# Where the high and low parts of rotated queries and keys are formed in a fused attention and MoE kernel

## Chip, cores and metric

The kernel runs on one core of a Trainium2 chip. The metric is the device time of one execution in microseconds (us), as a median over runs. Engines are named as in the profile: PE (TensorE; PEld is its weight load), DVE (VectorE), ACT (ScalarE), POOL (GpSimd), SP (SyncE, here only a queue of DMA issues).

## What is computed

Three stages follow each other. Attention with rotary embedding over 4 batches, 8 heads, 576 positions and head size 64; then a two-matrix MoE layer; then a gated one (SiLU). All is float32.

```
q_rot, k_rot = (rotate(q), rotate(k))
scores = scale * np.matmul(q_rot, k_rot.transpose(0, 1, 3, 2))
...
return np.matmul(attn, v).astype(np.float32)
...
h = x @ w_in
g = s * (np.maximum(h, 0.0) ** 2) + b
x = g @ w_out
...
silu = g * (1.0 / (1.0 + np.exp(-g)))     # g = x @ w_gate
return (silu * val @ w_out).astype(np.float32)   # val = x @ w_val
```

## The kernel before

Every matmul that must keep float32 accuracy is made from a high part (the value rounded to fp32r) and a low part (value minus high part), and the products high x high, high x low and low x high are summed in PSUM. So each operand is split once: one operation rounds it, a second subtracts.

The 32 heads are worked in 16 pairs. For each pair `prep(p)` makes the operands and `pair(p)` computes. `prep` loads q and k of two heads side by side into a tile `x` (two buffers; 128 x 1152 float32) and rotates them with four GpSimd operations (L486, L488, L491, L494, tile `ry` for the products). Then, in G = 3 groups of 384 columns, TensorE transposes the rotated rows into a PSUM bank `pst` (L514, nine transposes a pair; pool `t` of three banks, which the transposes of the probabilities, `ps_t`, use too). After a transpose the queries lie on partitions 0 to 63 and the keys on 64 to 127; a scale per partition (`qs`) gives the queries their factor. For pairs 2 to 15 each group's bank is read twice: ACT writes the rounded high part into `qkhi` (L523), and DVE subtracts it from the scaled bank into `qklo` (L525), which frees the bank. `qkhi` and `qklo` have one buffer each. Ten DMAs of SP then spread the two tiles into the operands `a`, `t` and `kz` of that pair (L547; two buffers of each, by parity of the pair), and only when they have landed may the next pair's high part be written. Pairs 0 and 1 take another way (L533, L536), which stays as it is.

`pair(p)` has nine units. Each computes scores of 128 rows on TensorE (`ps_s`, L619), a maximum on DVE (L622), and the exponential on ACT (L626). Three units make a third: their probabilities are transposed (L680, L683, banks `ps_t`), split into `ph` on ACT (L688) and `pl` on DVE (L695), and multiplied with the values (L710, L712), which GpSimd split (L569, L571, tile `vh`, three buffers). ACT takes the sum out (L723), and SP stores it (L731).

A pair has 40 score matmuls, 45 transposes of probabilities, 36 products with the values and 9 transposes of q and k: 130 on TensorE. Weights of the first MoE stage are loaded during attention and decoded (ACT L304, DVE L307, L310, L315) and split (ACT L342, GpSimd or DVE L349): the first WA = 10 of them have slots beside attention and their low part is GpSimd's; WB = 22 further slots open when attention is over.

The order of work on each engine is written out by a planner when the program is built: operations carry a duration, a priority (a smaller number first) and tokens for buffers, and `Schedule.run` plays them forward in planned time. On the chip every engine then runs its list strictly in that order, and an instruction whose semaphores are not there yet holds all that is behind it. The planner also keeps DVE operations marked `port=True` (the weight decode among them) from running while GpSimd is planned to be busy, and the other way round.

Of the kernel before, what the change touches and what calls it, by code (L numbers as in the profile page):

```python
# [8 lines left out]
F32 = mybir.dt.float32  # L9
# [21 lines left out]
class Schedule:  # L31
# [17 lines left out]
    def op(self, eng, dur, fn, prio, deps=(), acq=(), rel=(), lag=0.0, port=False):  # L49
        o = Op()  # L50
        o.size, o.next = None, []
        o.eng, o.dur, o.lag, o.fn, o.prio, o.port = eng, dur, lag, fn, prio, port
        o.acq, o.rel, o.users, o.ready, o.done = acq, rel, [], 0.0, None
        for t in rel:
            t.left += 1
        o.need = 0
        for d in set(d for d in deps if d is not None):
            d.users.append(o)
            o.need += 1
        self.ops.append(o)  # L60
        return o
# [116 lines left out]
def tile_attention_moe_moe(  # L178
# [26 lines left out]
    NU = PC  # L205
    QA = PC // 2
    UBS = (512, 512, 512, 384, 384)
    WA = 10
    WB = 22
    NE = 7  # L210
    LATE, LAST = 1 << 20, 1 << 21
    WARM = 75
# [9 lines left out]
    sch = Schedule()  # L222
    op = sch.op
    sch.free.update({
        "raw": 3, "dec": 2, "wa": WA, "x": 2, "vr": 2, "ry": 1, "hi": 1, "vh": 3, "opb0": 1, "opb1": 1, "l": 2, "lb": 2, "cr": 1, "e": NE, "ph": 2, "pl": 2,
        "xr": 2, "rbx": 1, "s": 2, "t": 3, "v": 1, "xhb": 1, "gb": 2, "rb2": 3,
    })

# [19 lines left out]
    ld_p = att.enter_context(tc.tile_pool(name="ld", bufs=2))  # L248
    vr_p = att.enter_context(tc.tile_pool(name="vr", bufs=2))
    rp_p = att.enter_context(tc.tile_pool(name="rp", bufs=1))  # L250
    v_p = att.enter_context(tc.tile_pool(name="v", bufs=3))
    ph_p = att.enter_context(tc.tile_pool(name="ph", bufs=2))
    pl_p = att.enter_context(tc.tile_pool(name="pl", bufs=2))
# [170 lines left out]
    def prep(p):  # L424
# [34 lines left out]
        def taken(ps):  # L459
            return ps[:, 0:CG].rearrange("p (h s) -> p h s", h=2)  # L460

        for g in range(G):
            cs = slice(g * PC // G, (g + 1) * PC // G)
            eng = "dve" if p == 0 else "pool"
            e = nc.vector if eng == "dve" else nc.gpsimd
            tt = t_dve if eng == "dve" else t_pool
            wide = [128, PC // G, 2, D // 2]
            def views(a, cs=cs):
                return st["x"].rearrange("p c j (a d) -> p c j a d", a=2)[:, cs, :, a], st["ry"][:, cs, :, a]
            def r0(g=g, e=e, views=views, cs=cs, wide=wide):  # L470
                if g == 0:
                    st["ry"] = rp_p.tile([128, PC, 2, 2, D // 2], F32, tag="ry", name="ry")
                e.tensor_tensor(out=views(0)[1], in0=views(1)[0], in1=rt[:, cs, 2:3].to_broadcast(wide), op=ALU.mult)
            def r1(e=e, views=views, cs=cs, wide=wide):
                e.tensor_tensor(out=views(1)[1], in0=views(0)[0], in1=rt[:, cs, 1:2].to_broadcast(wide), op=ALU.mult)
            def r2(e=e, cs=cs):
                xv = st["x"].rearrange("p c j (a d) -> p c (j a) d", a=2)[:, cs]
                e.tensor_tensor(out=xv, in0=xv, in1=rt[:, cs, 0:1].to_broadcast([128, PC // G, 4, D // 2]), op=ALU.mult)
            def r3(e=e, cs=cs):
                xv = st["x"].rearrange("p c j d -> p c (j d)")[:, cs]  # L480
                e.tensor_tensor(out=xv, in0=xv, in1=st["ry"].rearrange("p c j a d -> p c (j a d)")[:, cs], op=ALU.add)
            o = st.get("rope")
            if o is None and p:
                def y0():
                    st["ry"] = rp_p.tile([128, PC, 2, 2, D // 2], F32, tag="ry", name="ry")
                    nc.gpsimd.tensor_tensor(out=views2(0)[1], in0=views2(1)[0], in1=rt[:, :, 2:3].to_broadcast(whole), op=ALU.mult)  # L486
                def y1():
                    nc.gpsimd.tensor_tensor(out=views2(1)[1], in0=views2(0)[0], in1=rt[:, :, 1:2].to_broadcast(whole), op=ALU.mult)  # L488
                def y2():
                    xv = st["x"].rearrange("p c j (a d) -> p c (j a) d", a=2)  # L490
                    nc.gpsimd.tensor_tensor(out=xv, in0=xv, in1=rt[:, :, 0:1].to_broadcast([128, PC, 4, D // 2]), op=ALU.mult)  # L491
                def y3():
                    xv = st["x"].rearrange("p c j d -> p (c j d)")
                    nc.gpsimd.tensor_tensor(out=xv, in0=xv, in1=st["ry"].rearrange("p c j a d -> p (c j a d)"), op=ALU.add)  # L494
                n2 = PC * D
                for y, fn in enumerate((y0, y1, y2, y3)):
                    o = op("pool", t_pool(n2 if y < 2 else 2 * n2), fn, pr, (o, *lds[0], *rt_op), (ry_tok,) if y == 0 else (), (ry_tok,) if y == 3 else ())
                st["rope"] = o
            elif not p:
              o = None  # L500
              for y, fn in enumerate((r0, r1, r2, r3)):
                deps = [o, *lds[g], rt_op[g]]
                if y == 0 and g > 0:
                    deps.append(st["first"])
                o = op(eng, tt(fd if y > 1 else fd // 2), fn, pr + g, deps, (ry_tok,) if y == 0 and g == 0 else (),
                       (ry_tok,) if y == 3 else (), port=eng == "dve")
                if y == 0 and g == 0:
                    st["first"] = o
            ps_tok = Token("t")
            def tr(g=g):  # L510
                st["ps", g] = ps = ps_t.tile([128, 512], F32, tag="t", name="pst")
                rv = st["x"].rearrange("p c j d -> p c (j d)")
                for c in range(PC // G):
                    nc.tensor.transpose(taken(ps)[:, :, c * 64:(c + 1) * 64], rv[:, g * (PC // G) + c], ident.rearrange("p (h r) -> p h r", h=2))  # L514
            acq = (ps_tok, hi_tok if p > 1 else tok) if g == 0 else (ps_tok,)
            prt = pr + 3 + g
            o = st["tr"] = op("pe", 0.33, tr, prt, (o, eye_op, st.get("tr"), *(zeros[z] if p < 2 else ())), acq, (x_tok,))
            if p > 1:
                def hi(g=g):
                    if g == 0:  # L520
                        st["hi"] = rp_p.tile([128, 2 * S], F32R, tag="hi", name="qkhi")
                        st["lo"] = rp_p.tile([128, 2 * S], F32R, tag="lo", name="qklo")
                    nc.scalar.activation(out=place(st["hi"], g), in_=taken(st["ps", g]), func=AF.Copy, scale=qs_t)  # L523
                def lo(g=g):
                    nc.vector.scalar_tensor_tensor(  # L525
                        out=place(st["lo"], g), in0=taken(st["ps", g]), scalar=qs_t, in1=place(st["hi"], g).bitcast(F32), op0=ALU.mult, op1=ALU.subtract
                    )
                o = st["hi0"] = op("act", t_act(CG, True, 1), hi, prt, (o, qs_op, st.get("hi0")))
                trs.append(op("dve", t_dve(CG, 2), lo, prt, (o,), (), (ps_tok,)))
            else:  # L530
                def act(dst, rows, g=g):
                    scale = D ** -0.5 if rows is up else 1.0
                    return lambda: nc.scalar.activation(out=place(dst, g), in_=taken(st["ps", g])[rows], func=AF.Copy, scale=scale)  # L533
                def sub(dst, src, rows, g=g):
                    scale = D ** -0.5 if rows is up else 1.0
                    return lambda: nc.vector.scalar_tensor_tensor(  # L536
                        out=place(dst, g), in0=taken(st["ps", g])[rows], scalar=scale, in1=place(src, g).bitcast(F32), op0=ALU.mult, op1=ALU.subtract
                    )
                o1 = op("act", t_act(CG), act(t[dn], dn), prt, (o,))
                o2 = op("act", t_act(CG), act(a[up], up), prt, (o,))  # L540
                ops += [o1, o2, op("dve", t_dve(CG), sub(a[dn], a[up], up), prt, (o2,), (), (ps_tok,))]
                ops.append(op("act", t_act(CG), act(kz[up], dn), prt, (o,), (), (ps_tok,)))
                ops.append(op("dve", t_dve(CG), sub(t[up], t[dn], dn), prt, (o1,), (), (ps_tok,)))
        if p > 1:
            def sp(o, i, first=False):
                return sch.dma(
                    256 * o.shape[1], lambda: nc.sync.dma_start(out=o.bitcast(F32), in_=i().bitcast(F32)), pr + 6, (*trs, *zeros[z]),  # L547
                    (tok,) if first else (), (hi_tok,), pace=1.3
                )
# [821 lines left out]
```

## Time and profile before

| | |
|---|---|
| median of 3 runs | 1133.07 us (1133.0 to 1134.01) |
| span of the profiled execution, first to last instruction | 1130.5 us |
| mean granted clock of TensorE over the span | 0.995 of full speed |
| scores of pair 0 start, of pair 15 end | about 14 us, about 303 us |

The profile shows one execution from its first to its last instruction. Of that execution only the span is known; the median of the runs is 2.6 us above it, the time around the instructions.

### The profile page before, as it was taken

The numbers are of one execution on the slowest core, as the hardware profiler recorded it, in microseconds if no ns is written. First come the engines' busy times: TensorE is split into PE (matmuls) and PEld (weight loads), VectorE is DVE, ScalarE is ACT, GpSimd is POOL, SyncE is SP. The second block draws the span as 40 slices with busy tenths as digits, with TensorE's granted clock in tenths as the row PEclk, the third lists the DMA queues.
The fourth block names the chain that finished last, engine by engine and source line by source line (L and its number), as shares of the span: only waits on it lengthen the run. The fifth ranks groups of instructions, "written<-read, shape, count | busy, mean of one in ns | idle before, by whom it ended". The sixth has DMA issues, their size and how long they took to land. (4 is left out here: it accounts for less than half of the span.)

```text
span 1130.5 us, 17993 instructions
## 1 busy us (share of the span) xinstructions
PE 1103.6 (98%) x6314; PEld 1006.8 (89%) x6314; DVE 801.2 (71%) x1391; ACT 591.0 (52%) x1199; POOL 193.0 (17%) x156
## 2 busy tenths in 40 slices
PE   8989989999999999999999999999999999999998
PEld 7889888989988788888899999999979999899986
DVE  5879788999979867868768764555565555655560
ACT  5979888889978845544554543322242222422230
POOL 6876775752210000000000000000000000000000
PEclk9899999999999999999999999999999999999999
DMA  5587978777375477576576766766646652666501
GB/s 117 128 208 175 240 184 213 175 184 185 89 235 185 128 227 235 177 238 225 198 241 212 254 224 207 245 204 204 210 160 220 196 195 97 196 229 197 181 10 46
DMA packets 185721, 211.16 MB, mean 187 GB/s; under 512 B 71824, under 2 KB 121120, under 8 KB 185632
## 3 DMA queue, kind: packets, MB, share of 16 engines
q1 hardware_dynamic: 183792, 209.23, 61.8%
q8 instruction: 50, 0.82, 0.3%
q10 hardware_dynamic: 1840, 0.79, 0.2%
q14 instruction: 39, 0.32, 0.1%
HBM read 142.07 MB, written 47.26 MB: 167 GB/s over the span
## 5 line engine op out<-in xcount | busy, mean ns | idle before, releaser
L1241 DVE TENSOR_TENSOR tmp<-hb,tmp 128x384 f32<-128x384 f32 x252 | 140.0, 557 | 113.3 <-PE hb L811 112.4
L811 PE MATMUL hb<-xh,w 128*128 128x384 f32 (+1 forms) x560 | 199.2, 356 | 1.0 <-DVE w L349 1.0
L809 PE MATMUL hb<-xh,w 128*128 128x384 f32 (+1 forms) x560 | 199.0, 355 | 0.3 <-DVE pl L695 0.3
L810 PE MATMUL hb<-xl,w 128*128 128x384 f32 (+1 forms) x560 | 198.8, 355 | 0.0
L809 PE MATMUL acc<-gh,w 128*128 128x512 f32 (+1 forms) x320 | 117.8, 368 | 0.0
L810 PE MATMUL acc<-gl,w 128*128 128x512 f32 (+1 forms) x320 | 117.6, 368 | 0.0
L811 PE MATMUL acc<-gh,w 128*128 128x512 f32 (+1 forms) x320 | 117.6, 367 | 0.0
L622 DVE TENSOR_REDUCE nm<-ps_s 128x1 f32<-128x576 f32 x144 | 108.0, 751 | 9.8 <-PE ps_s L619 8.6
L809 PEld LDWEIGHTS hb<-xh,w 128*128 128x128 f32 x560 | 105.1, 188 | 10.9 <-PE ps_t L683 0.5
L810 PEld LDWEIGHTS hb<-xl,w 128*128 128x128 f32 x560 | 105.1, 188 | 10.3
L811 PEld LDWEIGHTS hb<-xh,w 128*128 128x128 f32 x560 | 105.1, 188 | 9.8 <-DVE w L349 1.8
L626 ACT ACTIVATE e<-ps_s,nm 128x576 f32<-128x576 f32 x144 | 107.3, 746 | 8.4 <-DVE nm L622 7.8
L688 ACT ACTIVATE ph<-ps_t 128x512 fp32r<-128x512 f32 x192 | 106.2, 574 | 10.1 <-PE ps_t L680 7.8
L619 PE MATMUL ps_s<-t,a 128*128 128x288 f32 x320 | 101.2, 332 | 7.2 <-ACT e L626 7.0
L710 PE MATMUL ps_av<-ph,vh 128*128 128x384 f32 (+1 forms) x320 | 97.9, 327 | 0.7 <-ACT xr L723 0.6
L695 DVE TENSOR_TENSOR pl<-ps_t,ph 128x512 fp32r<-128x512 f32 x144 | 95.9, 683 | 2.5 <-ACT ph L688 1.4
L1256 ACT ACTIVATE tmp<-tmp 128x384 f32<-128x384 f32 x72 | 37.8, 525 | 111.1 <-DVE tmp L1241 108.9
L680 PE MATMUL ps_t<-ident,e 128*128 128x128 f32 x576 | 87.7, 279 | 5.6 <-DVE qklo L525 4.0
L619 PE MATMUL ps_s<-kz,a 128*128 128x288 f32 x320 | 90.8, 299 | 0.0
L810 PE MATMUL hb<-w 128*128 128x384 f32 x264 | 88.9, 337 | 0.0
L811 PE MATMUL hb<-w 128*128 128x384 f32 x264 | 88.8, 337 | 0.0
L809 PE MATMUL hb<-w 128*128 128x384 f32 x264 | 88.5, 335 | 0.0
(117 smaller groups left out, 2304.2 us busy)
## 6 DMA issues: line engine op xcount, KB each, us to landing
w<-wd SPq DMA_DIRECT2D x120, 512.0 KB, 4.3
wd<-w SPq DMA_DIRECT2D x48, 512.0 KB, 3.6
raw<-in_moe_w_out_dram SPq DMA_DIRECT2D x28, 512.0 KB, 4.1
x_d<-xr SPq DMA_DIRECT2D x64, 144.0 KB, 2.7
w<-wd SPq DMA_DIRECT2D x36, 256.0 KB, 3.6
raw<-in_moe_w_in_dram SPq DMA_DIRECT2D x16, 512.0 KB, 4.4
raw<-in_moe_w_gate_dram SPq DMA_DIRECT2D x12, 512.0 KB, 5.5
raw<-in_moe_w_val_dram SPq DMA_DIRECT2D x12, 512.0 KB, 6.6
```

Source lines behind the costliest of these rows:

```text
L619: nc.tensor.matmul(ps[:, hf * 512:hf * 512 + HS], a[:, q0:q0 + 128], m[:, k0:k0 + HS], start=y == 0, stop=y == len(todo) - 1)
L622: nc.vector.tensor_reduce(out=st["nm"][:, u:u + 1], in_=st["s", u], axis=AX.XY, op=ALU.max, negate=True)
L626: nc.scalar.activation(out=st["e", u].rearrange("p (f n) -> p f n", f=2), in_=st["s", u], func=AF.Exp, bias=st["nm"][:, u:u + 1], accum_ou ...
L680: nc.tensor.transpose(ps[:, z * 128:z * 128 + 128], st["e", u][:, kc * 128:kc * 128 + 128], ident)
L688: nc.scalar.activation(out=st["ph", y][0:rows, 512 * i:512 * i + n], in_=st["pt", y, i][0:rows, 0:n], func=AF.Copy)
L695: nc.vector.tensor_tensor(out=dst, in0=st["pt", y, i][0:rows, 0:n], in1=st["ph", y][0:rows, c].bitcast(F32), op=ALU.subtract)
L710: nc.tensor.matmul(ps, vv, st["ph", y][:, c], start=kc == 0, stop=kc == 4)
L809: nc.tensor.matmul(o, lh, rh, start=first, stop=False)
L810: nc.tensor.matmul(o, lh, rl, start=False, stop=False)
L811: nc.tensor.matmul(o, ll, rh, start=False, stop=last)
L1241: nc.vector.tensor_tensor(out=st[dst, f], in0=ps[z], in1=st[a, f], op=ALU.add)
L1256: nc.scalar.activation(out=st[key, f], in_=st[key, f], func=AF.Silu)
```

## The change

For pairs 2 to 15 a transposed group leaves PSUM by one operation instead of two. It multiplies by `qs` and writes plain float32 back over the group's own columns of the tile `x`, which have just been transposed: on ACT for groups 0 and 2, on DVE for group 1. When the three groups are there, GpSimd makes the high part of all 1152 columns with one operation and the low part with another; the tile `x` is given back after the second, not after the transposes. `qkhi` and `qklo` get a pool of their own with two buffers each, and the token for a buffer is now taken by GpSimd's first operation, not by the first transpose. The scratch for DMA descriptors, which lies in SBUF, is set to 1 KB, and in the room so gained WA goes from 10 to 11 (WB, in the room that attention leaves, from 22 to 24).

```
-    WA = 10
-    WB = 22
+    WA = 11
+    WB = 24
...
-        "raw": 3, "dec": 2, "wa": WA, "x": 2, "vr": 2, "ry": 1, "hi": 1, ...
+        "raw": 3, "dec": 2, "wa": WA, "x": 2, "vr": 2, "ry": 1, "hi": 2, ...
...
+    hi_p = att.enter_context(tc.tile_pool(name="hi", bufs=2))
...
-            acq = (ps_tok, hi_tok if p > 1 else tok) if g == 0 else (ps_tok,)
+            acq = (ps_tok, tok) if g == 0 and p < 2 else (ps_tok,)
             prt = pr + 3 + g
-            o = st["tr"] = op("pe", 0.33, tr, prt, (...), acq, (x_tok,))
+            o = st["tr"] = op("pe", 0.33, tr, prt, (...), acq, (x_tok,) if p < 2 else ())
             if p > 1:
-                def hi(g=g):
-                    ...
-                    nc.scalar.activation(out=place(st["hi"], g), in_=taken(st["ps", g]), func=AF.Copy, scale=qs_t)
-                def lo(g=g):
-                    nc.vector.scalar_tensor_tensor(
-                        out=place(st["lo"], g), in0=taken(st["ps", g]), scalar=qs_t, in1=place(st["hi"], g).bitcast(F32), op0=ALU.mult, op1=ALU.subtract
-                    )
-                o = st["hi0"] = op("act", t_act(CG, True, 1), hi, prt, (o, qs_op, st.get("hi0")))
-                trs.append(op("dve", t_dve(CG, 2), lo, prt, (o,), (), (ps_tok,)))
+                def back(g=g):
+                    dst = st["x"].rearrange("p c j d -> p (c j d)")[:, g * CG:(g + 1) * CG]
+                    if g == 1:
+                        nc.vector.tensor_scalar(out=dst, in0=st["ps", g][:, 0:CG], scalar1=qs_t, scalar2=None, op0=ALU.mult)
+                    else:
+                        nc.scalar.activation(out=dst, in_=st["ps", g][:, 0:CG], func=AF.Copy, scale=qs_t)
+                dur = t_dve(CG, 1) if g == 1 else t_act(CG, True, 1)
+                trs.append(op("dve" if g == 1 else "act", dur, back, prt, (o, qs_op), (), (ps_tok,)))
...
         if p > 1:
+            def hi():
+                st["hi"] = hi_p.tile([128, 2 * S], F32R, tag="hi", name="qkhi")
+                st["lo"] = hi_p.tile([128, 2 * S], F32R, tag="lo", name="qklo")
+                nc.gpsimd.tensor_scalar(out=parts(st["hi"]), in0=val(), scalar1=1.0, scalar2=0.0, op0=ALU.mult, op1=ALU.add)
+            def lo():
+                nc.gpsimd.tensor_tensor(out=parts(st["lo"]), in0=val(), in1=parts(st["hi"]).bitcast(F32), op=ALU.subtract)
+            o = op("pool", t_pool1(2 * S), hi, pr + 5, trs, (hi_tok,))
+            trs = [op("pool", t_pool(2 * S), lo, pr + 5, (o,), (), (x_tok,))]
...
-    nc = _bacc.Bacc("TRN2", target_bir_lowering=False, num_devices=1)
+    nc = _bacc.Bacc("TRN2", target_bir_lowering=False, num_devices=1, dynamic_dma_scratch_size=1024)
```

## Rows read from the trace of the kernel before

**Rows 1.** Busy us of each engine, share of the span, instructions.

```profile
PE 1103.6 (98%) x6314; PEld 1006.8 (89%) x6314; DVE 801.2 (71%) x1391; ACT 591.0 (52%) x1199; POOL 193.0 (17%) x156
```

**Rows 2.** Busy by stretch: start:end, length, engines (xinstructions), clock, DMA share, GB/s.

```profile
60.00:90.00 30.00, 26.55 (x204) 25.12 (x204) 23.92 (x39) 23.59 (x56) 23.38 (x18) 1.00 0.82 194
90.00:120.00 30.00, 29.97 (x236) 28.52 (x235) 27.33 (x46) 26.97 (x66) 18.06 (x13) 1.00 0.84 216
...
270.00:300.00 30.00, 29.84 (x231) 28.39 (x230) 29.50 (x48) 28.70 (x69) 7.85 (x9) 1.00 0.55 142
...
30.00:300.00 270.00, 256.53 (x1931) 240.11 (x1932) 243.81 (x387) 236.05 (x559) 167.01 (x129) 0.99 0.76 182
300.00:390.00 90.00, 88.74 (x421) 73.50 (x421) 79.78 (x141) 74.12 (x132) 6.06 (x4) 1.00 0.59 180
```

**Rows 3.** TensorE's waits, 30 to 300 us: total us, times, longest.

```profile
PE ps_s L619 <- ACT e L626: 4.7, 8, 2.0
PE ps_t L680 <- DVE qklo L525: 4.0, 2, 2.6
PE pst L514 <- DVE qklo L525: 2.2, 2, 1.9
...
PE psr L646 <- DVE qklo L525: 0.9, 1, 0.9
```

**Rows 4.** Groups of ACT and DVE, 30 to 300 us, and two more waits of ACT.

```profile
L523 ACT ACTIVATE qkhi<-pst,qs 128x384 fp32r<-128x384 f32 x42 | 23.6, 582 | 16.9 <-DMA x_d<-xr 5.6 <-DMA kz<-qkhi 4.0 <-PE pst L514 3.0
...
L525 DVE SCALAR_TENSOR_TENSOR qklo<-pst,qs,qkhi 128x384 fp32r<-128x384 f32 x42 | 25.0, 613 | 13.4 <-ACT qkhi L523 10.4 <-DMA x_d<-xr 1.8 <-DMA rbx<-r_d 0.9
...
ACT qkhi L523 <- PE ps_s L619: 2.8, 2, 2.2
ACT qkhi L523 <- DMA rbx<-r_d: 1.4, 1, 1.4
```

**Rows 5.** Timeline around 135 us: start, us, engine, line, operation.

```profile
132.37 0.60 SPq L547 DMA_DIRECT2D kz<-qkhi  x1
...
135.20 1.05 ACT L523 ACTIVATE qkhi<-pst,qs 128x384 fp32r<-128x384 f32 x2 [4.01 <-DMA kz<-qkhi]
135.82 1.15 DVE L525 SCALAR_TENSOR_TENSOR qklo<-pst,qs,qkhi 128x384 fp32r<-128x384 f32 x2 [3.25 <-ACT qkhi L523]
...
136.49 1.18 PE L680 MATMUL ps_t<-ident,e 128*128 128x128 f32 x8 [2.63 <-DVE qklo L525]
```

**Rows 6.** Groups of GpSimd, 30 to 300 us.

```profile
L494 POOL TENSOR_TENSOR x<-x,ry 128x1152 f32<-128x1152 f32 x14 | 37.2, 2660 | 0.9
...
L571 POOL TENSOR_TENSOR vh<-vr,vh 128x320 fp32r<-128x320 f32 x29 | 26.5, 912 | 1.5
...
L486 POOL TENSOR_TENSOR ry<-x,rt 128x576 f32<-128x576 f32 x13 | 18.5, 1420 | 20.6 <-DMA x<-in_k_dram 19.1 <-issue 1.3
L569 POOL TENSOR_SCALAR vh<-vr 128x320 fp32r<-128x320 f32 x29 | 15.1, 520 | 51.1 <-PE ps_av L710 51.1
```

**Rows 7.** The page's group of DVE operations that read a 384-column PSUM bank.

```profile
L1241 DVE TENSOR_TENSOR tmp<-hb,tmp 128x384 f32<-128x384 f32 x252 | 140.0, 557 | 113.3 <-PE hb L811 112.4
```

**Rows 8.** Timeline, pair 2: its last split, its last spreading DMA, its first scores.

```profile
40.57 1.14 DVE L525 SCALAR_TENSOR_TENSOR qklo<-pst,qs,qkhi 128x384 fp32r<-128x384 f32 x2
...
47.98 1.34 SPq L547 DMA_DIRECT2D kz<-qkhi  x1
...
51.04 0.29 PE L619 MATMUL ps_s<-t,a 128*128 128x288 f32 x1
```

**Rows 9.** Timeline: end of one pair's rotation, and the transposes that follow it.

```profile
80.54 2.64 POOL L494 TENSOR_TENSOR x<-x,ry 128x1152 f32<-128x1152 f32 x1
...
96.47 0.71 PE L514 MATMUL pst<-ident,x 128*128 128x128 f32 x5
```

**Rows 10.** Two lines by instruction: ns min/median/max, first and last start.

```profile
L315 DVE SCALAR_TENSOR_TENSOR dec<-raw,dec x68: 680/691/1676, 225.8 to 654.8; 128x512 uint32<-128x512 uint32 x68
...
L349 POOL TENSOR_TENSOR w<-dec,w x10: 1285/1292/1774, 227.5 to 317.6; 128x512 fp32r<-128x512 f32 x10
```

More of the change, by code (lines that the diff above doesn't have):

```diff
@@ L224, in tile_attention_moe_moe @@
     sch.free.update({
-        "raw": 3, "dec": 2, "wa": WA, "x": 2, "vr": 2, "ry": 1, "hi": 1, "vh": 3, "opb0": 1, "opb1": 1, "l": 2, "lb": 2, "cr": 1, "e": NE, "ph": 2, "pl": 2,
+        "raw": 3, "dec": 2, "wa": WA, "x": 2, "vr": 2, "ry": 1, "hi": 2, "vh": 3, "opb0": 1, "opb1": 1, "l": 2, "lb": 2, "cr": 1, "e": NE, "ph": 2, "pl": 2,
         "xr": 2, "rbx": 1, "s": 2, "t": 3, "v": 1, "xhb": 1, "gb": 2, "rb2": 3,
@@ L514, in tr @@
                     nc.tensor.transpose(taken(ps)[:, :, c * 64:(c + 1) * 64], rv[:, g * (PC // G) + c], ident.rearrange("p (h r) -> p h r", h=2))
-            acq = (ps_tok, hi_tok if p > 1 else tok) if g == 0 else (ps_tok,)
+            acq = (ps_tok, tok) if g == 0 and p < 2 else (ps_tok,)
             prt = pr + 3 + g
-            o = st["tr"] = op("pe", 0.33, tr, prt, (o, eye_op, st.get("tr"), *(zeros[z] if p < 2 else ())), acq, (x_tok,))
+            o = st["tr"] = op("pe", 0.33, tr, prt, (o, eye_op, st.get("tr"), *(zeros[z] if p < 2 else ())), acq, (x_tok,) if p < 2 else ())
             if p > 1:
-                def hi(g=g):
-                    if g == 0:
-                        st["hi"] = rp_p.tile([128, 2 * S], F32R, tag="hi", name="qkhi")
-                        st["lo"] = rp_p.tile([128, 2 * S], F32R, tag="lo", name="qklo")
-                    nc.scalar.activation(out=place(st["hi"], g), in_=taken(st["ps", g]), func=AF.Copy, scale=qs_t)
-                def lo(g=g):
-                    nc.vector.scalar_tensor_tensor(
-                        out=place(st["lo"], g), in0=taken(st["ps", g]), scalar=qs_t, in1=place(st["hi"], g).bitcast(F32), op0=ALU.mult, op1=ALU.subtract
-                    )
-                o = st["hi0"] = op("act", t_act(CG, True, 1), hi, prt, (o, qs_op, st.get("hi0")))
-                trs.append(op("dve", t_dve(CG, 2), lo, prt, (o,), (), (ps_tok,)))
+                def back(g=g):
[6 more added lines that the diff above has]
+                trs.append(op("dve" if g == 1 else "act", dur, back, prt, (o, qs_op), (), (ps_tok,)))
             else:
@@ L544, in prep, with parts, val @@
         if p > 1:
+            def parts(x):
+                return x.rearrange("p (h g s) -> p h g s", h=2, g=G)
+            def val():
+                return st["x"].rearrange("p c j d -> p (c j d)").rearrange("p (g h s) -> p h g s", g=G, h=2)
+            def hi():
[6 more added lines that the diff above has]
+            trs = [op("pool", t_pool(2 * S), lo, pr + 5, (o,), (), (x_tok,))]
             def sp(o, i, first=False):
```

## Prediction, made before the changed kernel was run

> **What bounds the kernel now.** I read the page's busy times first. TensorE is busy 98% of the span [rows 1], so 26.9 us (1130.5 - 1103.6) is all the idle time that the profile admits, and a change that only moves work between other engines can win no more than TensorE loses by waiting or by lower clock.
>
> Next the busy time by stretch, to place that idle time. From 30 to 300 us, nearly all of attention, TensorE is idle 13.5 us of 270 (270 - 256.53); from 300 to 390 us 1.3 us of 90 [rows 2]. The change touches attention alone, apart from the slots for weights. The reader should look at the instruction counts beside the busy times, because a matmul's busy time overlaps its neighbour's and hides small holes. The densest stretch issues 236 matmuls in 30 us; 60 to 90 us issues 204 [rows 2]. At 236 per 30 us the 1931 matmuls of 30 to 300 us would need 245.5 us, so up to 24.5 us are lost there, visible or not (a little of it to clock, 0.99 in that row). Some records can be missing, so 24.5 is a ceiling. A pair has 130 matmuls: 18.2 us a pair now (270 x 130 / 1931), 16.5 us at the dense rate.
>
> Third, who TensorE waits for in those 270 us. In time 7.1 us ended with the low part: 4.0 + 2.2 + 0.9 us, of transposes that want a PSUM bank which `qklo` still holds. Another 4.7 us ended with an exponential [rows 3]. And why was `qklo` late? ACT stands idle 16.9 us in front of `qkhi`, and DVE 13.4 us in front of `qklo`, of which 10.4 for `qkhi` [rows 4]. The names that the view gives for ACT's waits differ (stores, spreading DMAs, scores), but the timeline shows one event: the last spreading DMA of the pair before is issued at 132.37, ACT gets to `qkhi` and stands 4.01 us until 135.20, DVE stands behind it, and TensorE loses 2.63 us until 136.49 [rows 5]. That is the single buffer of `qkhi`: it may not be written until the DMAs have read it. ACT's list is in order, so exponentials wait behind it.
>
> **What the change removes.** 42 reads of `qkhi` on ACT at 582 ns and 42 of `qklo` on DVE at 613 ns go [rows 4]: 24.4 and 25.7 us. In come 28 scaled copies on ACT, same source, size and scale, so 582 ns, 16.3 us; and 14 on DVE. A DVE operation of 384 columns from PSUM with a second input took 557 ns [rows 7]; with one input I take the same, 7.8 us. ACT is relieved by 8.1 us, DVE by 17.9 us over 14 pairs, about 0.6 and 1.3 us a pair.
>
> More important, the copy back waits only for its transposes. The wait for the spreading DMAs moves to GpSimd, which nothing in PSUM depends on, and with two buffers it is for the pair before last, some 18 us earlier. A bank is held for one operation instead of two in turn.
>
> Worth of this: at least the 7.1 us that end with `qklo`, plus 2.0 us, the longest wait for an exponential [rows 3], which in the timeline stood behind `qkhi` too: 9.1 us. At most ACT's idle time before `qkhi` except that for its own transposes, 5.6 + 4.0 + 2.8 + 1.4 = 13.8 us [rows 4]. I take 10.5, nearer the low end, since TensorE had work queued at the start of each stall (4.01 us of ACT became 2.63 us of TensorE).
>
> The lighter load of ACT and DVE may close some of the small holes: between 0 and 14 us (24.5 - 10.5). Where the stalls were short, in 270 to 300 us, 231 matmuls were issued with DVE busy 29.50 us of 30 [rows 2], within 0.6 us of the densest rate. So load by itself costs little; I take 2.
>
> **What it adds on GpSimd.** The low part is a two-input operation of 1152 columns like L494: 2660 ns. The high part is one-input like L569, which took 520 ns for 320 columns: in proportion to columns 1.87 us; growing as the two-input form does from 912 to 2660 ns, 1.52 us [rows 6]. I take 1.6, so 4.3 us a pair and 60 us for 14. GpSimd goes from 167.0 to 227 us busy of these 270 [rows 2], 84%. Per pair: rotation 8.2 us (2 x 1.42 + 2 x 2.66), values 2.9 us (two each of 0.520 and 0.912) [rows 6], and 4.3 us, 15.4 us against a period of 16.5 at best. It fits, with one microsecond over. What is behind a waiting GpSimd operation is the next rotation, and behind that the next pair's transposes on TensorE.
>
> The tile `x` is now held until the low part is made, so SP's next load of q and k waits some 6 us longer (1.2 for the last copy and its handover, 4.3, and part of a running operation). The cover: one rotation ended at 83.18 and its transposes came at 96.47 [rows 9], 13 us later, because the first of them also waited for the single `qkhi`. That token is gone from the transposes. I cost the longer hold at nothing; without that cover it would be up to 6 us in each pair where it fell.
>
> **What gets later.** Pair 2 has no such cover. Its split ended at 41.7, its last spreading DMA was issued at 47.98, and its first scores began at 51.04 [rows 8]. The chain grows by 4.3 us less the saved part of the last split. TensorE has transposes and products of pair 1 to fill in. Between 0 and 4.3 us; I take 1.5.
>
> The weights. Their decode is kept away from GpSimd's busy time by the planner, and GpSimd has 60 us more of it. In the trace the first of ten low parts was made at 227.5, the last at 317.6 [rows 10]: already at the edge, and the eleventh slot helps only if the decode keeps up. When it collides on the chip it costs: L315's longest took 1676 ns against a median of 691 [rows 10], about 1 us. Twenty-two such operations (two for each of eleven weights) each losing that would be 22 us of DVE; 300 to 390 us has 10.2 us of DVE free [rows 2], so at most 12 us, at least nothing. I take 1, as few decodes fall before pair 15's split is done.
>
> The Trainium skill, page SBUF — State Buffer, section Who interferes with whom, says that a VectorE instruction with two SBUF inputs and a GpSimd instruction that reads SBUF exclude each other: the later one waits for the whole of the earlier. The long L315 agrees. By that rule the decode pays for the new GpSimd work, which is the second rival below; the copies back, with one PSUM input, pay nothing.
>
> Descriptor scratch: all large queues of this kernel are issued by SP, none by GpSimd, and I cost the smaller scratch at nothing. The later stages have TensorE full, so more slots for weights buy nothing there.
>
> **Sum.** -10.5 - 2 + 1.5 + 1 = -10 us: a span of 1130.5 - 10 = 1120.5, and with the 2.6 us by which the median stands above the span, **1123 us**.
>
> **Rivals.** *GpSimd sets the pace* (slower). GpSimd now waits 51.1 us for `vh` buffers and 20.6 us for q and k [rows 6]. If those waits stay whole because its list is in order, 227 + 51.1 + 20.6 = 299 us is 29 us more than the 270 that there are; less the 12.5 us won, +16.5. It decides once more than 43 us of its waits remain (270 - 227). For it: 15.4 of 16.5 us a pair, and 19.1 of those 20.6 us end with loads, which now start later. Against it: the waits for `vh` end with TensorE's products, so they shrink when GpSimd itself is late. Middling case: +8, 1141 us.
>
> *Weights come late* (smaller gain). The mechanism above at 6 us instead of 1: 1128 us. For it: the late decode and the collision of [rows 10]; against it: DVE has 18 us more room in attention.
>
> *The stall only changes its name.* The copies wait for transposes that wait for a late rotation, or SP's queue, now holding loads until the low part is made, delays the stores and the spreading behind them. Then the 10.5 us come back elsewhere: 1133 us. Against it are the 13 us of cover [rows 9].
>
> **Chances.** Forecast 0.55 (its own range 1116 to 1129), GpSimd's pace 0.18 (1136 to 1150), late weights 0.15 (1124 to 1135), change of name 0.12 (1131 to 1136). A measurement of this kernel tells about 0.2%, 2.3 us, from no change: faster is below 1130.8, slower above 1135.3. Faster: nearly all of the first, most of the third, a little of the last, 0.68. Same: 0.13. Slower: the second and a tail, 0.19. The range from 1113 to 1139 leaves out the half of the slow rival that lies above 1139 and a few hundredths at the fast end, where the 14 us of small holes would close.
>
> **What would show it.** Right: ACT idle before the copies under 5 us in total, no wait of TensorE that ends with a q or k operation of more than 0.5 us, two operations a pair on GpSimd of about 1.6 and 2.7 us, GpSimd near 225 us busy up to 300 us, and scores of pair 15 ending some 10 us before 303. Wrong: waits of TensorE's `pst` transposes for GpSimd, idle time of GpSimd for q and k as large as before with scores spaced by over 18 us, scores waiting for the spreading DMAs, or MoE matmuls waiting for weights after attention. Most likely to mislead me is that the whole planned order shifts, so that stalls which no row of before shows appear.

## The result, and the profile after

The changed kernel took 1139.72 us (median of 4, 1139.25 to 1143.57) where the kernel before took 1133.54 us beside it: a ratio of 1.0063, 95% interval 1.0049 to 1.0078. It is slower by 6 us by the medians and by 7 us by the ratio; the forecast was 10 us faster, and the time lies just above the range. The profiled execution has a span of 1137.7 us, 7.2 more than before, and the last scores of pair 15 start at 310.8 us instead of 302.8. From there to the end 826.9 us pass, before it was 827.7: all of the loss arose in attention.

The page's busy times of the changed kernel, beside [rows 1]:

```profile
PE 1104.3 (97%) x6314; PEld 1012.0 (89%) x6314; DVE 795.3 (70%) x1362; ACT 587.4 (52%) x1185; POOL 247.5 (22%) x185
```

TensorE does the same work; GpSimd has 54 us more. By stretch, beside the last two of [rows 2]:

```profile
30.00:300.00 270.00, 249.79 (x1868) 237.96 (x1868) 225.85 (x343) 223.16 (x522) 213.34 (x152) 0.97 0.72 175
300.00:390.00 90.00, 88.29 (x444) 74.49 (x444) 84.30 (x143) 76.37 (x142) 13.63 (x10) 1.00 0.63 192
```

In 30 to 300 us 63 matmuls fewer were issued than before. At 130 a pair and the 16.5 us of the dense rate that is 8.0 us, the whole loss. After 300 us nothing is lost (444 matmuls instead of 421). ACT and DVE did get the relief that was predicted, and both stand idle more. The groups of the new operations in the same stretch (out<-in, count | busy, mean ns | idle time before it and what ended it), beside [rows 4] and [rows 6]:

```profile
L525 ACT ACTIVATE x<-pst,qs 128x384 f32<-128x384 f32 x28 | 16.3, 582 | 13.1 <-PE pst L515 5.1 <-POOL vh L580 4.0 <-POOL vh L582 3.3
...
L523 DVE TENSOR_SCALAR x<-pst,qs 128x384 f32<-128x384 f32 x14 | 8.6, 613 | 9.3 <-POOL vh L580 4.1 <-PE pst L515 4.1 <-issue 1.1
...
L552 POOL TENSOR_TENSOR qklo<-x,qkhi 128x1152 fp32r<-128x1152 f32 x14 | 38.0, 2711 | 0.2
...
L487 POOL TENSOR_TENSOR ry<-x,rt 128x576 f32<-128x576 f32 x13 | 18.4, 1418 | 23.7 <-DMA x<-in_k_dram 16.8 <-DMA x_d<-xr 6.7
L550 POOL TENSOR_SCALAR qkhi<-x 128x1152 fp32r<-128x1152 f32 x14 | 17.0, 1215 | 9.3 <-ACT x L525 8.5 <-DMA t<-qkhi 0.7
```

The durations are near those predicted. ACT no longer waits for a spreading DMA before it empties a bank. It still stands idle 13.1 us before its copies. The `vh` operations named there only ran beside them: the copies at 84.07, 119.25 and 236.73 us started right behind transposes that had waited for a rotation. What is new is in front of L487, the first operation of a rotation: 23.7 us. [Rows 6] shows 20.6 us there too, so the number alone says little; who waits behind it does. TensorE's waits, beside [rows 3] (total us, times, longest):

```profile
PE pst L515 <- POOL x L495: 7.9, 4, 3.3
PE ps_s L630 <- ACT e L637: 4.4, 5, 2.3
PE ps_t L694 <- DVE pl L706: 3.4, 3, 2.0
PE ps_t L691 <- ACT x L525: 3.2, 1, 3.2
```

The 7.1 us that ended with `qklo` are gone, and 7.9 us that end with the rotation (L495) stand in their place: TensorE now reaches the transposes before the rotated tile is there. The last row is another event. It ends with a copy, but that copy stood in ACT's list behind the decode of a weight that came late (ACT, then TensorE):

```profile
186.67 0.66 ACT L305 ACTIVATE dec<-raw 128x512 f32<-128x512 f32 x1 [3.91 <-DMA raw<-in_moe_w_out_dram]
...
187.85 0.66 PE L691 MATMUL ps_t<-ident,e 128*128 128x128 f32 x4 [3.18 <-ACT x L525]
```

One round of a tile `x`, from a timeline of SP, GpSimd and TensorE (start, us; L393 loads, L487 to L495 rotate, L515 transposes, L550 and L552 split, L558 spreads):

```profile
86.53 0.60 SPq L393 DMA_DIRECT2D x<-in_q_dram  x1
...
91.59 1.43 POOL L487 TENSOR_TENSOR ry<-x,rt 128x576 f32<-128x576 f32 x1 [1.58 <-DMA x_d<-xr]
...
98.25 2.67 POOL L495 TENSOR_TENSOR x<-x,ry 128x1152 f32<-128x1152 f32 x1
...
100.98 0.87 PE L515 MATMUL pst<-ident,x 128*128 128x128 f32 x6 [0.52 <-POOL x L495]
...
109.23 1.15 POOL L550 TENSOR_SCALAR qkhi<-x 128x1152 fp32r<-128x1152 f32 x1
...
112.99 2.65 POOL L552 TENSOR_TENSOR qklo<-x,qkhi 128x1152 fp32r<-128x1152 f32 x1
...
115.67 0.49 SPq L558 DMA_DIRECT2D a<-qklo  x1
...
122.60 0.60 SPq L558 DMA_DIRECT2D kz<-qkhi  x1
123.31 0.61 SPq L393 DMA_DIRECT2D x<-in_q_dram  x1
```

From load to next load of the same tile (pairs 6 and 8) 36.8 us pass, 18.4 us a pair with two tiles: 5.1 us until the rotation begins, 9.3 for it, 8.3 for transposes, copies and the wait in GpSimd's list, 6.4 for the split, and 7.7 more because the next load stands in SP's list behind the spreading DMAs of this pair. Parts of the round are waits, so it does not tell by itself whether it sets the pace or follows it; the experiments decide that. In the kernel before, the transposes at 96.47 [rows 9] were soon followed by the next load of their tile:

```profile
101.25 0.56 SPq L392 DMA_DIRECT2D x<-in_q_dram  x1
```

Over the twelve such loads of each trace, from the first transposes of pairs 2 to 13 to the next load, 4.3 us pass on average before the change (1.3 to 7.3) and 19.1 us after it (14.9 to 22.3). The other tile's rotation ended at 118.21 in this trace, and TensorE began its transposes at 118.26 after 3.27 us of idle time; behind it the granted clock was half, as in two later stretches of 3.4 us:

```profile
117.40:124.20 6.80, 5.94 (x26) 5.92 (x27) 1.97 (x3) 2.51 (x6) 5.65 (x7) 0.50 0.85 198
```

From 60 to 300 us the mean granted clock is 0.97, where before it was 1.00; from 30 to 60 us it is 0.94 against 0.89. That makes, as an estimate from these rounded clocks, 240 x 0.03 - 30 x 0.05 = some 5.7 us of lost clock (0.01 is 2.4 us in the longer stretch; half is 1.2 instead of 2.4 GHz). TensorE's idle time in 30 to 300 us grew beside it from 13.5 to 20.2 us (270 - 249.79). Together that is more than the 8.0 us lost, so some of the hidden holes of [rows 2] must have closed; no row shows them one by one.

### The profile page after: what moved, and what is told of

Its sections match the earlier page's. It is cut to its first block, busy times and chain, and to the rows that moved or that the text cites. A ratio compares the mean times of both kernels' runs of the same rounds, so it can differ in the third digit from the quotient of the medians.

```text
span 1137.7 us, 17994 instructions
## 1 busy us (share of the span) xinstructions
PE 1104.3 (97%) x6314; PEld 1012.0 (89%) x6314; DVE 795.3 (70%) x1362; ACT 587.4 (52%) x1185; POOL 247.5 (22%) x185
## 4 chain that ended last, share of the span: by engine, by line
PE 85%; DVE 4%; ACT 3%; DMA 2%; issue 2%; POOL 2%; SPq 1%; POOLq 0%; ACTq 0%; DVEq 0%
PE hb L822 14%; PE hb L821 14%; PE hb L820 14%; PE acc L820 6%; PE acc L822 6%; PE acc L821 6%; PE ps_s L630 4%; PE acc L1184 4%; PE acc L1185 4%; PE acc L1186 4%; PE ps_t L691 3%; PE ps_av L721 2%; PE ps_av L723 2%; DVE nm L633 1%; ACT e L637 1%
## 5 line engine op out<-in xcount | busy, mean ns | idle before, releaser
L821 PEld LDWEIGHTS hb<-xl,w 128*128 128x128 f32 x560 | 105.1, 188 | 10.5
L721 PE MATMUL ps_av<-ph,vh 128*128 128x384 f32 (+1 forms) x320 | 100.7, 335 | 1.1 <-DVE ph L706 0.9
```

The costliest lines, as they stand in the source:

```text
L721: nc.tensor.matmul(ps, vv, st["ph", y][:, c], start=kc == 0, stop=kc == 4)
L821: nc.tensor.matmul(o, lh, rl, start=False, stop=False)
```

## The experiments

The theories named in the expectations: *Hold*, the tile `x` is given back late and its round sets the pace; *Load*, GpSimd has too much work; *Cover*, only the slack in front of the transposes is missing. Each ratio is against the kernel before on the same chip.

**One part alone: two buffers for `qkhi` and `qklo`, with the old split on ACT and DVE.**

```
+    hi_p = att.enter_context(tc.tile_pool(name="hi", bufs=2))
+    nc = _bacc.Bacc(..., dynamic_dma_scratch_size=1024)
```

> The old way out of PSUM (high part on ACT, low part on DVE), with two buffers of qkhi and qklo in the room of the smaller scratch; slots for weights as before. If the single buffer was what held ACT (the prediction's first step), ACT's idle time before qkhi falls from 16.9 us to under 6 us and the time to 1122 to 1127 us. If the wait for the buffer was also the slack that kept TensorE's transposes of q and k behind the rotation (theory Cover), those transposes now wait for GpSimd and the gain is under 3 us: 1131 to 1135 us.

1138.27 us, ratio 1.0036 (1.0022 to 1.0049): outside both ranges. The 16.9 us of ACT in front of `qkhi` shrank to 8.3, not under 6, and yet the kernel is slower: one stall of 7.7 us is left, and TensorE stands behind it (waits of ACT, then of TensorE, 30 to 300 us):

```profile
ACT qkhi L524 <- DMA x_d<-xr: 7.9, 2, 7.7
...
PE ps_t L681 <- DVE qklo L526: 7.6, 2, 7.4
```

The granted clock was half in three stretches, 17 us together. A second buffer alone gains nothing. TensorE does not wait for the rotation here, as *Cover* had it, but the slack in front of the transposes shrank: for pairs 2 to 7 they start 0.8 to 4.8 us after the rotation's end, where before it was 5.1 to 18.3 us.

**The other part alone: small scratch and one and two more slots for weights.**

```
+    WA = 11
+    WB = 24
```

> The kernel before, with only the smaller scratch and the 11 and 24 slots for weights. Cover and the theory that GpSimd is simply too full (Load) both expect no difference, 1132 to 1135 us. If slots or scratch made the changed kernel slow, 1137 us or more.

1131.73 us, 0.9975 (0.9964 to 0.9986). The room costs nothing.

**GpSimd's work alone: the kernel before, and two operations a pair of the same size on tiles that nobody reads.**

> The kernel before, with two more GpSimd operations in pairs 2 to 15, of the kind and size that the change adds (128 x 1152, one input, then two), on tiles of their own that nothing else reads. Load: GpSimd's 53 us more by themselves cost most of the 7 us, 1138 us or more. Hold: GpSimd has room, 1132 to 1136 us.

1130.63 us, 0.9979 (0.9967 to 0.9991), with GpSimd as busy as after the change:

```profile
30.00:300.00 270.00, 256.87 (x1960) 243.28 (x1960) 244.75 (x388) 238.18 (x563) 213.96 (x155) 0.99 0.74 179
```

*Load* does not hold in the kernel before: the same 214 us of GpSimd with 92 matmuls more than in the changed kernel. The own tile below shows the same with the split on GpSimd (215.0 us, 1959 matmuls).

**Less work in front of the transposes: the product with the cosine (L492) left out, so queries and keys are not scaled by it.**

```
-                for y, fn in enumerate((y0, y1, y2, y3)):
+                for y, fn in ((0, y0), (1, y1), (3, y3)):
```

> The changed kernel without the rotation's product with the cosine (x is left unscaled there), 2.67 us less of GpSimd in each pair from the second on. Load: GpSimd falls from 15.3 to 12.6 us a pair and the loss goes: 1123 to 1130 us, and no wait of TensorE's transposes for the rotation above 1 us. Cover: the planner knows of the shorter rotation and again puts the transposes at its planned end, so waits of 4 us or more for the rotation stay: 1132 to 1138 us.

1134.5 us, 0.9999 (0.9989 to 1.001). Taking 2.7 us out of the round takes the loss away, not more. Neither theory holds whole: TensorE has no wait for the rotation left, as *Load* said, but the time is in *Cover*'s range. By *Hold*'s arithmetic (2.7 us shared by two tiles, 14 pairs) it would have been 19 us, so the round is not all that limits.

**More slack for the transposes: the planner is told that the rotation is ready 5 us later.**

> The changed kernel with the same instructions; only the planner is told that the rotation of pairs 2 to 15 is ready 5 us later than it plans its last operation to end, so TensorE's transposes of q and k stand later in its list. Cover: TensorE's 7.9 us of waits for the rotation go to under 2 us, the clock stays up after 60 us, and the time falls to 1122 to 1130 us. Load: GpSimd does as much as before and pairs come later still: 1139 us or more.

1166.27 us, 1.0283 (1.0263 to 1.0303). *Cover* falls: TensorE's waits for the rotation are gone, and yet the time rises. The transposes now start 6.6 us after the rotation on average instead of 1.6; that holds the tile 5 us longer, and the pace drops to 1731 matmuls (the time lies in *Load*'s range too; the run of GpSimd's work alone speaks against that theory):

```profile
30.00:300.00 270.00, 243.19 (x1731) 228.41 (x1731) 215.92 (x323) 209.10 (x489) 210.15 (x148) 0.93 0.69 165
```

Against the changed kernel it lost some 25 us (1.0283 / 1.0063), 1.8 us for each of 14 pairs; *Hold* gives 2.5 (5 us shared by two tiles).

**The load ahead of the spreading DMAs in SP's list.**

> The changed kernel with one priority changed: the load of q and k for the pair after next stands ahead of the spreading DMAs in SP's list when its tile x comes free. Hold: the round of a tile falls by the 7 us of the spreading issues, from 37 to about 31 us, and the time to 1128 to 1136 us. Load: 1138 us or more.

1144.67 us, 1.0101 (1.0087 to 1.0116): worse, and a miss for *Hold*. TensorE's waits for the rotation are down to 1.4 us, but now the list of SP stands at a load whose tile is not free (7.6 us, twice) while other transfers wait behind it; TensorE's longest wait, 10.2 us, ends with an exponential behind a late weight. So moving the load within one in-order list is no cure.

**A third tile `x` (and ten slots instead of eleven, for the room).**

> The changed kernel with three tiles x instead of two (and 10 slots for weights beside attention, to make room). Theory Hold: the loss comes from the tile x, which the change keeps until the low part is made and whose next load then stands behind ten spreading DMAs in SP's list; two tiles go round in about 37 us, 18.5 us a pair. With three, the spreading DMAs of pairs 6 to 15 land 6 us or more before their scores, as they did before the change, and the time is 1128 to 1135 us. Load (GpSimd is too full): no gain, 1138 us or more.

1133.14 us, 1.0005 (0.9992 to 1.0017): the loss is gone, as *Hold* had it. GpSimd has no wait of over 0.5 us for a load of `x` left between 60 and 300 us. One stall of 8.7 us remains, for a weight.

**The copies go to a tile of their own, so `x` is free after the transposes (ten slots).**

```
-                    dst = st["x"].rearrange("p c j d -> p (c j d)")[:, g * CG:(g + 1) * CG]
+                    if g == 0:
+                        st["bk"] = rp_p.tile([128, 2 * S], F32, tag="bk", name="bk")
+                    dst = st["bk"][:, g * CG:(g + 1) * CG]
...
-            trs = [op("pool", t_pool(2 * S), lo, pr + 5, (o,), (), (x_tok,))]
+            trs = [op("pool", t_pool(2 * S), lo, pr + 5, (o,), (), (bk_tok,))]
```

> The changed kernel, but the scaled copies go into a tile of their own (one buffer, in the room of the eleventh slot), so x comes free after the transposes as before the change; GpSimd's work is the same. Hold: 1128 to 1135 us, with the spreading DMAs landing 5 us or more before the scores. Load: 1138 us or more.

1128.72 us, 0.9955 (0.9939 to 0.997): faster than both kernels, as *Hold* had it. GpSimd waits for no load of `x` from 60 to 300 us. Rotation, transposes and next load of one tile:

```profile
90.74 2.65 POOL L495 TENSOR_TENSOR x<-x,ry 128x1152 f32<-128x1152 f32 x1
...
94.97 0.82 PE L515 MATMUL pst<-ident,x 128*128 128x128 f32 x6
...
98.88 0.60 SPq L393 DMA_DIRECT2D x<-in_q_dram  x1
```

From first transposes to next load 3.9 us pass on average, as before the change. But the transposes start only 2.5 us after the rotation's end on average (0.5 to 5.8), where in the kernel before it was 14.1 us (5.1 to 20.8). The slack in front of the transposes is gone here too, although no tile `x` is held longer.

One large stall is left in the profiled execution (1132.0 us). The timeline of SP, ACT and TensorE:

```profile
141.82 0.52 SPq L562 DMA_DIRECT2D a<-qkhi  x1
...
149.24 0.59 SPq L562 DMA_DIRECT2D kz<-qkhi  x1
149.88 0.59 SPq L292 DMA_DIRECT2D raw<-in_moe_w_in_dram  x1
...
155.19 0.66 ACT L305 ACTIVATE dec<-raw 128x512 f32<-128x512 f32 x1 [9.74 <-DMA raw<-in_moe_w_in_dram]
...
157.11 0.61 PE L634 MATMUL ps_s<-t,a 128*128 128x288 f32 x1 [8.40 <-ACT e L641]
```

The first weight is loaded behind ten spreading DMAs, its decode stands first in ACT's list, and exponentials wait behind it. The granted clock is 0.52 from 153.4 to 163.6 us.

**Slack for the weights.** In all kernels that follow, the planner is told that a weight's load in attention is ready some time later than it plans; nothing else changes.

```
+            if prio == TP * NP:
+                o = op("sp", 0.0, lambda: None, prio, (o,), lag=12.0)
```

With 12 us, for the own tile, the kernel before, the changed kernel and the one with three tiles:

> The kernel with an own tile for the copies, and the planner told that the weights loaded during attention are ready for their decode 12 us later than it thinks; instructions are the same. In the run without it ACT stood 9.7 us before the first weight's decode, TensorE lost 8.4 us of that and then ran 10.2 us at half clock, worth 5.1 us. If that one wait is what is left (theory Hold plus one late load), it goes and the time is 1113 to 1121 us. If the stalls only move on to another wait (theory Shuffle: any new order has its own stalls of this size), 1126 us or more.

> The kernel before with the same 12 us for the decode of the weights. There ACT waited 1.1 us for such a load, so both theories expect 1131 to 1135 us; a gain of 4 us or more would say that the slack helps by itself and not through the own tile.

> The changed kernel with the same 12 us for the decode. ACT waited 4.6 us in all for such loads there (3.9 and 0.7); Hold expects at most that back, 1135 to 1140 us, since tile x still sets the pace. Below 1131 us would say that late loads and not the tile were the loss.

> Three tiles x with the same 12 us for the decode. ACT waited 8.7 us for the first weight there, TensorE 8.7 us behind it, and 10.2 us went at half clock. Hold plus one late load: 1116 to 1124 us. Shuffle: 1130 us or more.

1134.5 us, 1.0017 (1.0003 to 1.0032); 1138.82 us, 1.0048 (1.003 to 1.0066); 1147.76 us, 1.0127 (1.0112 to 1.0143); 1142.51 us, 1.0079 (1.0066 to 1.0093). All four lose against the same kernel without slack. The first and the last lie in *Shuffle*'s range; for the kernel before and the changed one every range was missed. With the own tile the last scores of attention start at 292.0 us instead of 299.0, but the MoE stage then starts without its weights:

```profile
300.00:330.00 30.00, 25.24 (x108) 19.89 (x108) 17.49 (x28) 18.18 (x31) 5.48 (x4) 0.99 0.62 184
330.00:360.00 30.00, 27.89 (x110) 22.16 (x109) 28.88 (x52) 23.70 (x42) 1.74 (x1) 0.90 0.64 187
```

The kernel before had 163 and 134 matmuls in these stretches. So 12 us is too much for the eleven weights there. The kernel before with 12 us shows no such gap (168 and 134); ACT's idle time in front of `qkhi` grew from 16.9 to 21.0 us instead, and why was not followed. Two smaller doses for the own tile, 12 us for the first weight alone, and 5 us for all:

> The kernel with its own tile for the copies, and the planner is told that the load of the first weight alone is ready 12 us later than it plans; the other ten weights are planned as they were. Theory One load: what keeps the gain at 5 us instead of 10 is one late event, the decode that waits 9.7 us for the first weight, with TensorE's 8.4 us of idle time behind it. Part of that idle time is work that is done sooner elsewhere, and the 5.1 us of half clock go with it. Expected 1119 to 1125 us, no wait of ACT for a raw weight above 2 us, no half clock between 140 and 170 us. Rival Order: every new order of the lists brings such an event at another place; then 1127 to 1134 us, the wait at 150 us gone and another of over 4 us elsewhere. Rival Weights: slack for one weight already makes the MoE start late; then TensorE issues under 115 matmuls in 300 to 330 us, and the time is 1129 us or more.

> The same kernel, all eleven weights of attention planned with 5 us of slack, instead of 12 that gave 1134.5 us with attention 7 us shorter and a MoE start that waits for weights. Theory One load: 5 us cover about half of the 9.7 us wait, so a wait of 3 to 5 us stays in front of the first decode, and the MoE start loses less than with 12 us: 1124 to 1130 us. Rival Order: 1127 to 1136 us with stalls of over 4 us at other places of attention. Rival Weights: the loss at the MoE start comes with any slack for all eleven, 1131 us or more with under 110 matmuls in 300 to 330 us.

The first: 1132.99 us, 0.9998 (0.9986 to 1.001). The stall moved to the second weight, so *Order* holds for it:

```profile
162.98 0.66 ACT L307 ACTIVATE dec<-raw 128x512 f32<-128x512 f32 x1 [8.17 <-DMA raw<-in_moe_w_out_dram]
...
164.42 0.61 PE L636 MATMUL ps_s<-t,a 128*128 128x288 f32 x1 [8.00 <-ACT e L643]
```

The second: **1124.89 us, 0.9925 (0.9909 to 0.9942)**, the fastest of all and within *One load*'s range, though the wait of 3 to 5 us that it expected in front of the first decode is not there. No wait of TensorE is over 2.0 us in 30 to 300 us, and it issues 113 matmuls more there than the changed kernel:

```profile
30.00:300.00 270.00, 258.09 (x1981) 245.51 (x1981) 239.01 (x368) 236.66 (x557) 215.92 (x157) 0.99 0.74 180
```

Two controls with the same 5 us: the kernel before with the slots, and the changed kernel as it was.

> Control: the kernel before with the small scratch and the slots (which took 1131.7 us, 0.9975), and the planner told that the eleven weights of attention are ready 5 us later. Theory Change works: the 1124.9 us of the kernel with an own tile and the same slack come from the way in which queries and keys leave PSUM; slack alone gives the old way nothing, because its stalls are those for the single qkhi buffer: 1129 to 1135 us, ACT still idle over 10 us in front of qkhi. Rival Slack alone: late loads of weights were a hidden loss of the kernel before too, and the old way with slack comes to 1123 to 1127 us; then the change itself is worth nothing even with its own tile.

> Control: the changed kernel as it is (copies written back into the tile of queries and keys), with the same 5 us of slack for the eleven weights. Theory Hold: the tile that is held until the low part is made sets the pace, and slack for weights doesn't touch it: 1134 to 1142 us, spreading DMAs of the later pairs landed no more than 3 us before the pair's scores, more than two stretches of half clock or waits of TensorE for transposes that stand at the end of the rotation. Rival Slack alone: the late loads were what cost the changed kernel its gain, 1123 to 1129 us.

1137.91 us, 1.0048 (1.0034 to 1.0062), and 1138.29 us, 1.0056 (1.0041 to 1.0071). Slack alone gives neither anything. The kernel before with the slots loses 0.7% by it (from 0.9975), more than either theory had; ACT stands 20.7 us in front of `qkhi`. The changed kernel stays where it was (1.0063), in *Hold*'s range, and ACT waits for no weight there any more: so the one late weight of the changed kernel was not what made it slower. The waits of GpSimd (60 to 300 us) and of TensorE in the changed kernel with slack:

```profile
POOL ry L489 <- DMA x<-in_k_dram: 22.7, 7, 5.0
...
POOL ry L489 <- DMA x_d<-xr: 5.9, 2, 4.3
...
PE pst L517 <- POOL x L497: 9.3, 5, 2.6
```

and the only wait of GpSimd for `x` in the own-tile kernel with the same slack:

```profile
POOL ry L489 <- DMA x<-in_k_dram: 4.4, 3, 2.8
```

## Why the prediction was wrong

**The step that failed** is "I cost the longer hold at nothing". Three pairs of kernels differ in whose tile the copies go to, in one slot, and in the lists that the planner makes from that. From own tile to tile `x` the time rises by 1.08% without slack (1.0063 / 0.9955), by 1.32% with 5 us (1.0056 / 0.9925), by 1.10% with 12 us (1.0127 / 1.0017): some 12, 15 and 12 us. The third tile `x` takes 0.58% off without slack and 0.47% with 12 us (1.0063 to 1.0005, 1.0127 to 1.0079). Two errors lie in the step. The 13 us between a rotation and its transposes [rows 9] were taken for cover; they were slack that stood behind the single `qkhi`, and they went when it went: from 14.1 us on average to 2.5 us with the own tile, where `x` is free after the transposes. The same paragraph says so of the token without drawing the conclusion. And the longer hold was put at some 6 us by adding durations; it measured 14.8 us on average (19.1 - 4.3). In the timeline above 22.3 us pass from the first transposes to the next load of the tile: beside the 6.4 us of the split, 8.3 us until GpSimd's list comes to it, and 7.7 us in SP's list after it.

**From the forecast to the result.** The forecast was -10 us. With the own tile, where the hold does not grow, the change gave -5 us (0.9955). By the pair without slack the hold added 12 us to that, which makes the measured +7. Why it was -5 and not -10 without the hold is open; the stall behind the late weight is one candidate.

**The removed stall** was there: after the change the waits for `qklo` and for the spreading DMAs are gone, and none of TensorE's ends with the split on GpSimd. That it was worth 10.5 us is not shown. The two buffers alone lost 4 us, so the stall at its place was not simply 10 us to be had. With the tile free and 5 us of slack for the weights the whole change gives 8.4 us (1133.32 to 1124.89), close to the sum of 10. But that is the best of four lists of the own-tile kernel; the mean of their ratios is 0.9974, a gain of 3 us, no more than slots alone gave the kernel before. The best list issues 1981 matmuls in 30 to 300 us where the dense rate of the prediction, 236 in 30 us, would make 2124.

**The terms of the sum.** High and low part: 1.22 and 2.71 us on average, predicted 1.6 and 2.66. Copies: ACT 582 ns as predicted, DVE 613 instead of 557; ACT relieved by 7.3 us (predicted 8.1), DVE by 16.4 (predicted 17.9). Pair 2 began its scores at 55.1 instead of 51.0 us, 4 us later where 1.5 was taken and 4.3 was the upper end. The weights cost nothing after 300 us, but one was late in attention. GpSimd 213.3 us busy up to 300 us, predicted near 225. The time around the span was 1.8 us in the profiled execution (1139.48 - 1137.7), where 2.6 was added.

**The rivals.** *GpSimd sets the pace* gave the right side and a range that holds the time, but by the wrong mechanism: as much work more costs the kernel before nothing, and its waits for `vh` fell from 51.1 to 9.1 us as the counter-argument said. *The stall only changes its name* had the mechanism, a late rotation and loads that SP holds until the low part is made, at 1133 us: it gave back the gain and stopped there, as if the new stall could be no longer than the old one. *Weights come late* shows once in the changed kernel, in the wait of 3.2 us above with 3.4 us of half clock behind it, and it is what 12 us of slack does to the own tile. Its collision is visible: L316, the decode's last operation, has a median of 691 ns; of three before 300 us two took 1852 and 1240 ns while GpSimd read SBUF. That agrees with the rule on the shared port that the prediction took from the Trainium skill, page SBUF — State Buffer, section Who interferes with whom.

**The signs that it named.** Of those for right, the two new operations and GpSimd's busy time came about. ACT's idle time before the copies was 13.1 us instead of under 5, waits of TensorE that end with a q or k operation made 11.1 us (7.9 + 3.2, where 7.1 had been), and attention ended 8 us later instead of 10 earlier. Of those for wrong, the waits of `pst` for GpSimd and the idle time of GpSimd for q and k came true.

**What stays open.** Every new list brings stalls of its own. Four lists of the own-tile kernel, which differ only in what the planner believes of the weights, gave 1124.9, 1128.7, 1133.0 and 1134.5 us; slots or idle work alone made the kernel before 0.21 to 0.25% faster. So a single pair of kernels does not size a mechanism below some 10 us; the cost of the hold rests on three pairs that agree, on the third tile and on the waits for loads. No list that writes the copies back into one of two tiles `x` was below 1.0056 (0.9999 without the cosine product, which is less work), and no list of the own tile above 1.0017. Why two buffers alone lose 4 us was not settled, and whether 5 us is the best slack was not tried further.

## What to carry to other kernels

When a stall is removed, the slack that stood behind it goes as well: measure the cover of every other chain without the stall, not beside it. A buffer's hold is the whole round from load to next load, with the waits in each in-order list (here two, GpSimd's and SP's), and with two buffers the period is at least half of it; compare that with the rate that is wanted, and give a third buffer or another tile for a trial to see whether the round sets the pace or follows it. If a change writes its result back into its input's tile, price a tile of its own first.

## What the runs showed of the hardware

GpSimd's one-input operation on 1152 columns took 1.156 us in the median and the two-input one 2.668 us, a ratio of 2.3, where 320 columns showed 520 and 912 ns, 1.75 [rows 6]; the prediction's two extrapolations, 1.52 and 1.87 us, were both too high.

SP took about 0.6 us for each spreading DMA, so that ten held its list for 7 to 8 us (141.82 to 149.83 in the own-tile kernel) while a load behind them needed 5 us from issue to use. The Trainium skill, page DMA: Bandwidth & Descriptors, section Issuing engines are not separate DMA queues, says that the time to start a DMA is usually small relative to the DMA itself. For one alone that agrees here (0.6 against 5 us), but ten short ones ahead of a load took longer than the load.

In the changed kernel waits of TensorE of 2.2, 3.2 and 3.3 us were followed by 3.4, 3.4 and 6.8 us at half clock (0.50 to 0.51 granted), and the wait of 8.4 us in the own-tile kernel went with 10.2 us (0.52). A wait of 2.3 us in the changed kernel (until 264.55) and one of 2.6 us in the kernel before [rows 5] were followed by none (1.00). A short wait can so cost half as much to as much again in clock, or nothing.
